# A weight group moved to ScalarE's DMA queue, and scores held until a chunk's first gate/up step

## The chip, the cores and the metric

The kernel runs on one core of one Trainium2 chip. The metric is the device time of one execution in microseconds; the median of three runs before the change is 568.12 us (567.70 to 568.79).

## The reference

The input x has 2048 tokens of width 576, in bf16. It is layer-normalised once, and two branches read the result: sliding-window attention (32 heads of 18, each token sees itself and the 255 tokens before it) and a gated feed-forward of inner width 4608.

```python
xn = _layernorm(x, axis=-1)
# attention
qkv = xn @ wqkv                       # 576 -> 3 x 576, 32 heads of 18
p = softmax(where(mask, q k^T * 18**-0.5, -1e9))
s = (p @ v) @ wo
# feed-forward
h = sigmoid(xn @ w_gate) * (xn @ w_up)   # 576 -> 4608
g = silu(h @ w_down)                     # 4608 -> 576
out = x + s * g
```

## The kernel before

**Tiling.** The tokens are done in four chunks of 512. For each chunk the kernel normalises and transposes x (`build_ln`), projects to q, k and v (`build_qkv`, matmuls on L465), and then runs the gate/up product of the feed-forward (`build_ffn`, L810), into which it weaves the attention of the same chunk: score units on L594 with their exps on ScalarE (L612), and "pv" steps, probabilities times values, on L663. Then come the attention's output product (L740) and the down product (L930). The 4608 inner columns are 36 tiles of 128, numbered from 0. One tile is 9 contraction steps, and in each step TensorE runs two matmuls side by side on its two row halves, the gate's on the lower and the up's on the upper: 18 matmuls a tile. A finished tile goes through a tanh on ScalarE (L824) into `tring`, and DVE multiplies it with the up half into `hT` (L828). Gate and up tiles use PSUM banks 4 to 7, one each, so tile n+2 needs the banks of tile n back.

**Weights.** Three gate/up tiles make a weight group. `load9` loads a group in four pieces (240, 192, 192 and 240 KB) into one of `RW` = 3 slots of `wgs`; the group after the third waits for the slot of the first, which is free when TensorE has finished tile 2. In the code `fg == RW` is this fourth group, group 3, needed from tile 9 on. At tile `XS[c]` (10 in chunk 0, 1 in the others) two of the gate's steps are done on the upper half, with their weights loaded apart into `sat` (`load_x`, "wx0"); from there on the gate of a tile ends two steps ahead of its up. A second such load, "wx1", serves the last tile.

**Queries and keys in chunk 0.** Each of the four 128-token blocks of q and of k is projected, copied to `pk` or, when that is full, to a buffer of `expr`, and then turned by a DMA transpose into `qkp` (`build_qk`, DMA line L213; plain DMAs are L214). The eight transposes go out in the order q0 q1 q2 k0 k1 q3 k2 k3, behind the third weight group (`QKT_BEHIND`). A unit of scores needs some of them; the first in TensorE's order has 16 matmuls and needs q1, q2, q3, k1 and k2.

**The order of the work.** Every DMA of the kernel before is issued from SyncE (SP). The order on each engine comes from a planner in the kernel, `schedule`. It keeps a clock for each engine and takes, on each engine, the ready operation with the least (start + 40 ns times its `prio`); a score unit has prio 1, a gate/up step 3. A DMA occupies its issuer for a fixed issue time. Its data pass through one line for all DMAs in the order of planning: it begins when the line is free, and at the earliest 1600 ns (`DMA_LAT_NS`) after its issue, and takes its (weighted) bytes at 320 a nanosecond; what needs it is ready `slack` (600 ns here) after that. `odeps` order two operations in the plan without a semaphore, `deps` with one. `emit` then writes the programs and gives every operation that somebody waits for a semaphore count; each DMA lane has a semaphore of its own. The plan's times only set the order; the chip follows the semaphores.

Due times of the plan for the kernel before, in us of the plan's clock, for following the order:

| operation | planned |
|---|---|
| third weight group, last piece landed | 26.89 |
| transposes issued, first to last | 18.84 to 27.94 |
| transpose of k2 landed, with slack | 36.10 |
| tanh of tile 2 done | 29.15 |
| gate/up tile 5 ends, tile 6 begins | 34.14 |
| first score unit starts (behind tile 6) | 36.10 |

Of the kernel before, what the change touches and what calls it, by code (L numbers as in the profile page):

```python
# [12 lines left out]
P = 128  # L13
# [21 lines left out]
RW = 3  # L35
# [10 lines left out]
RTH = 2  # L46
RREC = 2
RBN = 4
XS = (10, 1, 1, 1)
XP = (4, 0)  # L50
RUN = 3
WX_PRIO = -1
WX_FT = 7
QKV_FIRST = "q0 q1 v0 v1 q2 v2 k0 v3 k1 q3 k2 k3"
QKV_NEXT = "q0 k0 q1 v0 v1 k1 q2 k2 v2 q3 k3 v3"
QKV_GATE = 2
# [17 lines left out]
W_ISSUE_NS = 660.0  # L74
# [2 lines left out]
LATE_SLACK = 5000.0  # L77
LN_STEP = 1
XT_CUT = 4
QKT_BEHIND = {2: 0}  # L80
WARM = 10
X0_SLACK = 0.0
# [4 lines left out]
W_FACTOR = 1.42  # L87
X0_FACTOR = 1.7
XT_BYTES = 1.2
XT0_BYTES = 1.5  # L90
W0_FACTOR = 1.5
DMA_LAT_NS = 1600.0
DMA_BYTES_PER_NS = 320.0
# [6 lines left out]
def act_ns(n):  # L100
    return n / 1.2 + 80.0


def dve_ns(n, rate=1.0):
    return n / (0.96 * rate) + 75.0
# [68 lines left out]
class Builder:  # L174
# [173 lines left out]
            return r  # L348
        self.op_warm = self.pe(n * WARM_NS, f, name, deps=deps, prio=-9, psum=[ps])

    def load9(self, low, up, w_low, w_up, name, lane, deps, prio, factor):
        cols = w_low.shape[1]
        a = w_low.rearrange("(j p) c -> p j c", p=64)
        b = w_up.rearrange("(j p) c -> p j c", p=64)
        out = []
        for k, (dst, src, n) in enumerate(((low[:, 0:5, :], a[:, 0:NC:2, :], 5), (up[:, 0:4, :], b[:, 1:NC:2, :], 4),
                                           (low[:, 5:NC, :], a[:, 1:NC:2, :], 4), (up[:, 4:NC, :], b[:, 0:NC:2, :], 5))):
            out.append(self.dma(dst, src, factor * n * 64 * cols * 2, f"{name}.{k}", lane + (k,), deps=deps, prio=prio,
                                issue=W_ISSUE_NS))
        return out  # L360

    def build_weights(self):
# [399 lines left out]
    def load_x(self, c):  # L762
        self.sx, dx = self.r_s.take()
        f = XS[c] * P
        src = [(self.wg, f, 1, 64), (self.wu, (NFT - 1) * P, 0, 0)]
        self.op_wx = []
        for n, (w, f, j, r0) in enumerate(src):
            a = w[:, f:f + P].rearrange("(j p) c -> p j c", p=64)[:, j:j + 3:2, :]
            dst = self.sat[r0:r0 + 64, self.sx, 0:2 * P].rearrange("p (j c) -> p j c", j=2)
            self.op_wx.append(self.dma(dst, a, 2 * W_FACTOR * 64 * 2 * P * 2, f"wx{n}:{c}", ("wx", n), deps=dx, prio=WX_PRIO))  # L770
            self.r_s.release(self.sx, self.op_wx[-1])

    def build_ffn(self, c):
        pg = [Psum((6,), (7,), (5,), (4,)) for _ in range(NFT)]
        pu = [Psum((6,), (7,), (5,), (4,)) for _ in range(NFT)]
        slots, dmas = {}, {}
        xs, xe = XS[c], NFT - 1
        gp = [i for i in range(NC) if LO[i] not in UP[0:2]]
        up = [i for i in range(NC) if UP[i] not in LO[0:2]]
        low, high = [], []  # L780
# [3 lines left out]
        n = NC * (xs - 1) + XP[0]  # L784
        high[n:n] = [(0, xs, 0, 0), (0, xs, 1, 1)]
        n = len(low) - NC + XP[1]
# [27 lines left out]
        for n in range(len(low)):  # L814
            for half, st in enumerate((low, high)):
                gu, ft, i, x = st[n]
                count[(gu, ft)] = count.get((gu, ft), 0) + 1
                flags[(half, gu, ft, i)] = (count[(gu, ft)] == 1, count[(gu, ft)] == NC)

        def finish(ft):  # L820
            st_, dt_ = self.r_t.take()

            def f_th(e, ps=pg[ft]):
                return e.activation(self.tring[:, st_, :], self.bank(ps), ACTF.Tanh, scale=0.5)  # L824
            th = self.rd("ACT", act_ns(CH), f_th, f"th:{c}:{ft}", deps=[tile_end[(0, ft)]] + dt_, prio=1, psum=[pg[ft]])

            def f_mul(e, ps=pu[ft]):
                return e.scalar_tensor_tensor(self.hT[:, ft, :], self.tring[:, st_, :], 1.0, self.bank(ps),  # L828
                                              ALU.add, ALU.mult)
            war = [self.f2_last[ft // WDG]] if self.f2_last else []  # L830
            mul = self.rd("DVE", dve_ns(CH), f_mul, f"hm:{c}:{ft}", deps=[th, tile_end[(1, ft)]] + war, prio=1,
                          psum=[pu[ft]])
            self.r_t.release(st_, mul)
            self.op_hT[ft] = mul
# [6 lines left out]
        for n0, n1 in zip(cuts, cuts[1:]):  # L841
            deps, alloc, fence, done, ended = [prev], [], None, [], []
            for n in range(n0, n1):
                for half, st in enumerate((low, high)):
                    gu, ft, i, x = st[n]
                    fg = ft // FG
                    if x is None and fg not in slots:
                        sw, dw = self.r_w.take()
                        slots[fg] = sw
                        wp = W_PRIO[fg] if c == 0 and fg < RW else -2  # L850
                        fc = slice(fg * FG * P, (fg + 1) * FG * P)
                        ws = self.load9(self.wgs[0:64, sw, :, :], self.wgs[64:P, sw, :, :], self.wg[:, fc],
                                        self.wu[:, fc], f"w:{c}:{fg}", ("w", sw),
                                        dw + ([self.w_gate] if c > 0 and fg < RW else []), wp,
                                        W0_FACTOR if c == 0 and fg < 5 else 1.42)
                        dmas[fg] = ws
                        if c == 0 and fg == RW:
                            self.op_wx[1].add_dep(self.op_f1[(0, WX_FT)])
                        if c == 0 and fg in QKT_BEHIND:
                            for o in self.op_qkt[QKT_BEHIND[fg]:]:  # L860
                                o.behind = ws[-1:]
                    key = (gu, ft)
                    if key not in seen:
                        seen.add(key)
                        alloc.append((pg, pu)[gu][ft])
                        if self.f2_last and gu == 0:
                            deps.append(self.f2_last[ft // WDG])
                    if x is None:
                        deps += dmas[fg]
                        group_left[fg] -= 1  # L870
                        if group_left[fg] == 0:
                            ended.append(fg)
                    else:
                        deps.append(self.op_wx[gu])
                    if half != gu or key in ((0, xs), (1, xe)):
                        if tile_last.get(key, (half,))[0] != half:
                            fence = tile_last[key][1]
                    left[key] -= 1
                    if left[key] == 0:
                        done.append(key)  # L880
            if not prev:
                deps += self.all_xn

            def f(e, n0=n0, n1=n1):
                for n in range(n0, n1):
                    step(e, 0, *low[n])
                    r = step(e, 1, *high[n])
                return r
            o = self.pe((n1 - n0) * mm_ns(CH), f, f"f:{c}:{low[n0][1]}:{n0}", deps=deps, prio=3, psum=alloc, mode="r64")
            if fence:  # L890
                o.add_dep(fence)
                o.fence = fence
            for n in range(n0, n1):
                for half, st in enumerate((low, high)):
                    gu, ft = st[n][:2]
                    tile_last[(gu, ft)] = (half, o)
                    users = (pg, pu)[gu][ft].users
                    if users[-1] is not o:
                        users.append(o)
            for fg in ended:  # L900
                self.r_w.release(slots[fg], o)
            for key in done:
                tile_end[key] = o
                if key[0] == 0:
                    self.op_f1[(c, key[1])] = o
                if tile_end.get((1 - key[0], key[1])):
                    finish(key[1])
            prev = o
        for o in self.op_se:
            o.add_dep(prev)  # L910
        mms = [prev]
# [4 lines left out]
        for blocks in (((0, 1), (2,), (3,)) if c == 0 else ((0,), (1,), (2,), (3,))):  # L916
# [5 lines left out]
            for q in range(NWD):  # L922
                for i in blocks:
                    def f_f2(e, q=q, i=i, ps=banks[i]):
                        b = ps.banks[0] * 512
                        for fl in range(WDG):
                            ft = q * WDG + fl
                            lhsT = self.hT[:, ft, i * P:(i + 1) * P]
                            for n0, n1 in ((0, 512), (512, D)):
# [3 lines left out]
                    deps = [self.op_hT[ft] for ft in range(q * WDG, (q + 1) * WDG)] + [self.op_wd[q]]  # L933
                    o = self.op("PE", WDG * (mm_ns(512) + mm_ns(64)), f_f2, f"f2:{c * QPC + i}:{q}", deps, 3,
                                alloc=[banks[i]] if q == 0 else [], mode="full",
                                odeps=prev + ([self.op_wop[i - RTH]] if q == 0 and i >= RTH else []))
# [189 lines left out]
    def emit(self):  # L1126
# [8 lines left out]
        lane_cnt = [0] * len(lanes)  # L1135
        cnt = {e: 0 for e in ENGS}
        for e in ENGS:
            for o in self.prog[e]:
                if not o.needs_tok:
                    continue  # L1140
                if o.lane is not None:
                    ln = self.lane_ids[o.lane]
                    lane_cnt[ln] += 16
                    o.tok = (("L", ln), lane_cnt[ln])
                else:
                    cnt[e] += 1
                    o.tok = (("E", e), cnt[e])

        def semof(key):
            return lanes[key[1]] if key[0] == "L" else self.sem[key[1]]  # L1150
# [94 lines left out]
```

## Time and profile before

| what | value |
|---|---|
| median of three runs | 568.12 us |
| the profiled execution, its own time | 567.65 us |
| its span, first to last instruction | 565.0 us |
| granted TensorE clock | 0.999 |
| score units, L594 | 32.4 us of TensorE |
| down product, L930 | 131.0 us of TensorE |
| tanh, L824 | 144 of 600 ns on ScalarE |
| exp, L612 | 152 of 1022 ns on ScalarE |
| DMA moved over the span | 73.29 MB, mean 130 GB/s |

The profile is of one execution, and its times are us from the span's first instruction. Rows of a timeline give start, length, engine, line, operation, what is written from what, and a count; in brackets stands the idle time of that engine ahead of the row and what ended it by the profile. Engine names: PE is TensorE's matmuls, ACT ScalarE, DVE VectorE, SPq the queue of SyncE, which issues DMAs. A DMA row's length is the time of its issue, not of the transfer; "to landing" is from the issue's start to the last byte's semaphore.

### The profile page before, as it was taken

How to read it: one execution, taken by the hardware profiler on the slowest of the kernel's cores; microseconds unless marked ns; L12 is line 12 of the kernel's file. 1: busy time of each engine (PE TensorE's matmuls, PEld its weight loads, DVE VectorE, ACT ScalarE, POOL GpSimd, SP SyncE). 2: the span in 40 equal slices, each digit the busy share in tenths (PEclk: the TensorE clock that was granted, in tenths of full speed). 3: DMA queues.
4: the chain of work that ended last, by engine and by line, in shares of the span. 5: the costliest groups of instructions: out<-in, count | busy, mean ns of one | idle time of the engine just before them, and what ended most of it. 6: DMA issues, size and time to landing. Idle time of an engine off the chain costs nothing.

```text
span 565.0 us, 17870 instructions
## 1 busy us (share of the span) xinstructions
PE 555.0 (98%) x7830; PEld 283.0 (50%) x7854; DVE 307.4 (54%) x664; ACT 274.6 (49%) x372; POOL 28.2 (5%) x55
## 2 busy tenths in 40 slices
PE   8999999999999999999999999999999999999997
PEld 5634444457544444456654444445665444444544
DVE  6136987741136886772204778767121586686213
ACT  7456665514146947721407576580220855855011
POOL 3000001010000100010000011001000000000100
PEclk9999999999999999999999999999999999999999
DMA  8999999628956665324794665713559355660001
GB/s 200 219 187 249 231 224 215 136 62 114 181 105 148 151 151 135 86 52 83 106 210 109 144 153 122 161 36 71 89 124 206 87 126 129 147 131 23 20 22 43
DMA packets 126026, 73.29 MB, mean 130 GB/s; under 512 B 54782, under 2 KB 125438, under 8 KB 125950
## 3 DMA queue, kind: packets, MB, share of 16 engines
q1 hardware_dynamic: 125950, 72.16, 62.0%
q8 instruction: 62, 1.02, 0.8%
q14 instruction: 14, 0.11, 0.1%
HBM read 55.48 MB, written 2.36 MB: 102 GB/s over the span
## 4 chain that ended last, share of the span: by engine, by line
PE 94%; SPq 2%; DMA 1%; issue 1%; DVE 1%; ACT 0%
PE ps L810 50%; PE ps L930 23%; PE ps L465 8%; PE ps L594 5%; PE ps L663 4%; PE ps L740 3%; SPq L214 2%; PE ps L960 2%; DMA wqkv_sb<-in_A_wqkv_dram 1%; ACT sat L755 0%; ACT expr L612 0%; DVE tf L679 0%; DVE hT L828 0%; DVE pk L681 0%; DVE tf L684 0%
## 5 line engine op out<-in xcount | busy, mean ns | idle before, releaser
L810 PE MATMUL ps<-xn,wgs 64*128 64x512 bf16 x2576 | 296.3, 377 | 1.4 <-ACT expr L612 1.4
L810 PEld LDWEIGHTS ps<-xn,wgs 64*128 64x128 bf16 x2576 | 119.4, 94 | 143.7 <-issue 8.9
L612 ACT ACTIVATE expr<-ps 128x1024 bf16<-128x1024 f32 x152 | 147.2, 1022 | 26.3 <-PE ps L594 26.1
L930 PE MATMUL ps<-wd_sb,hT 128*128 128x64 bf16 (+1 forms) x1056 | 131.0, 284 | 2.2 <-issue 1.0
L824 ACT ACTIVATE tring<-ps 128x512 bf16<-128x512 f32 x144 | 86.3, 600 | 82.8 <-PE ps L810 80.6
L828 DVE SCALAR_TENSOR_TENSOR hT<-tring,ps 128x512 bf16<-128x512 bf16 x144 | 97.9, 680 | 30.6 <-ACT tring L824 14.2
L930 PEld LDWEIGHTS ps<-wd_sb,hT 128*128 128x128 bf16 x1080 | 68.1, 98 | 65.0 <-issue 1.4
L630 DVE TENSOR_TENSOR expr<-expr,m 128x512 bf16<-128x512 bf16 (+2 forms) x152 | 58.5, 412 | 55.5 <-ACT expr L612 54.5
L991 ACT ACTIVATE thf<-ps 128x576 bf16<-128x576 f32 (+2 forms) x17 | 10.6, 622 | 135.5 <-PE ps L930 128.3
L993 DVE SCALAR_TENSOR_TENSOR thf<-thf,ps 128x576 bf16<-128x576 bf16 (+2 forms) x17 | 12.2, 719 | 106.5 <-ACT thf L991 106.5
L465 PE MATMUL ps<-wqkv_sb,xn 64*128 64x288 bf16 x864 | 54.7, 283 | 0.5 <-ACT xn L454 0.2
L465 PEld LDWEIGHTS ps<-wqkv_sb,xn 64*128 64x128 bf16 x864 | 42.9, 94 | 11.2 <-issue 1.8
L594 PEld LDWEIGHTS ps<-qkp 18*64 18x64 bf16 x1472 | 16.2, 103 | 32.6 <-ACT expr L612 14.0
L594 PE MATMUL ps<-qkp 18*64 18x320 bf16 (+4 forms) x1472 | 32.4, 259 | 0.1
L641 POOL COPY qkp<-qkp 128x256 bf16<-128x256 bf16 x24 | 9.8, 410 | 288.1 <-PE ps L594 288.1
L513 DVE CAST pk<-ps 128x576 bf16<-128x576 f32 x15 | 11.3, 755 | 23.1 <-PE ps L465 22.9
L703 DVE STREAM_TRANSPOSE op__63<-pk 128x512 bf16<-128x512 bf16 x32 | 22.3, 698 | 0.2
L663 PEld LDWEIGHTS ps<-expr,vau 64*32 64x32 bf16 x1440 | 18.0, 92 | 7.6 <-issue 4.9
L681 DVE STREAM_TRANSPOSE pk<-ps 128x512 f32<-128x512 f32 x32 | 21.5, 673 | 0.0
L663 PE MATMUL ps<-expr,vau 64*32 64x320 bf16 (+5 forms) x1440 | 20.9, 253 | 0.3
L740 PE MATMUL ps<-wo_sb,oT 64*128 64x512 bf16 (+1 forms) x288 | 18.7, 283 | 0.1
L679 DVE STREAM_TRANSPOSE tf<-ps 128x512 f32<-128x512 f32 x16 | 11.5, 716 | 11.8 <-PE ps L663 11.8
(54 smaller groups left out, 197.1 us busy)
## 6 DMA issues: line engine op xcount, KB each, us to landing
wgs<-in_B_w_gate_dram SPq DMA_DIRECT2D x48, 240.0 KB, 3.9
wgs<-in_B_w_up_dram SPq DMA_DIRECT2D x48, 240.0 KB, 4.9
wgs<-in_B_w_up_dram SPq DMA_DIRECT2D x48, 192.0 KB, 4.0
wgs<-in_B_w_gate_dram SPq DMA_DIRECT2D x48, 192.0 KB, 4.8
wd_sb<-in_B_w_down_dram SPq DMA_DIRECT2D x9, 576.0 KB, 8.2
xf<-in_A_x_dram SPq DMA_DIRECT2D x18, 144.0 KB, 2.2
out_dram<-xf SPq DMA_DIRECT2D x15, 144.0 KB, 2.0
xr<-in_A_x_dram SPq DMA_DIRECT2D x14, 144.0 KB, 4.7
```

What stands on the lines that cost most here:

```text
L465: r = e.matmul(self.bank(ps, HV, hf), self.xn[r0:r0 + 64, k, i * P:(i + 1) * P], self.wqkv_sb[r0:r0 + 64, j, k, :], start=(k == 0), stop=( ...
L594: r = e.matmul(self.ps[64 * half:64 * half + 64, b:b + n * 64], self.qkp[r0:r0 + DH, hg, k0:k0 + 64], self.qkp[r0:r0 + DH, hg, q0 * 64:(q0 ...
L612: return e.activation(self.expr[:, es, 2 * pr:2 * pr + 2, :], src, ACTF.Exp, scale=SM_SCALE)
L630: return e.tensor_tensor(ap, ap, m, ALU.mult)
L663: r = e.matmul(self.ps[32 * j:32 * j + 32, b + q0 * 64:b + (q0 + n) * 64], vf[:, v0:v0 + 32], self.expr[p0:p0 + 64, es, j, pos * 64:(pos + ...
L681: t3 = self.rd("DVE", dve_ns(CH), lambda e, tg=tg, hg=hg: e.transpose(tg, self.bank(ps2[hg][1])), f"t3:{c}:{hg}", deps=[o, self.last_mul] ...
L703: t2 = self.op("DVE", dve_ns(CH), lambda e, on=on: e.transpose(self.op_[:, hg % NOT, :], on.rearrange("p g d -> p (g d)")), f"t2:{c}:{hg}" ...
L740: r = e.matmul(self.bank(ps2[w], n1 - n0, n), self.oT[r0:r0 + 64, kt, qi * P:(qi + 1) * P], self.wo_sb[r0:r0 + 64, kt, n0:n1], start=(swap ...
L810: return e.matmul(self.bank((pg, pu)[gu][ft]), w, self.xn[r0:r0 + 64, i, :], start=first, stop=last, tile_position=(r0, 0))
L824: return e.activation(self.tring[:, st_, :], self.bank(ps), ACTF.Tanh, scale=0.5)
L828: return e.scalar_tensor_tensor(self.hT[:, ft, :], self.tring[:, st_, :], 1.0, self.bank(ps), ALU.add, ALU.mult)
L930: r = e.matmul(self.ps[:, b + n0:b + n1], lhsT, self.wd_sb[:, q, fl, n0:n1], start=(ft == 0), stop=(ft == NFT - 1))
```

## The change

Group 3 of chunk 0 is issued from ScalarE: the first two pieces are ordered after the tanh of tile 2, the other two after that of tile 3. `XS[0]` goes from 10 to 13, and wx0 now waits for the end of gate tile 5 (wx1 for that of tile 7, as before). The planner's byte factor for the transposes of chunk 0, `XT0_BYTES`, goes from 1.5 to 1.2. In chunks 1 to 3 every score unit is ordered after the chunk's first gate/up step (`SC_GATE`). Semaphore counts of DMA lanes are given in the order of the plan over all engines, since a lane may now be used from two engines.

```diff
-XS = (10, 1, 1, 1)
+XS = (13, 1, 1, 1)
-WX_FT = 7
+SC_GATE = 0
-XT0_BYTES = 1.5
+XT0_BYTES = 1.2
@@ load9
-    def load9(self, low, up, w_low, w_up, name, lane, deps, prio, factor):
+    def load9(self, low, up, w_low, w_up, name, lane, deps, prio, factor, eng="SP"):
...
-                                issue=W_ISSUE_NS))
+                                issue=W_ISSUE_NS, eng=eng))
@@ build_ffn
+        ths = {}
...
+            ths[ft] = th
...
-                                        W0_FACTOR if c == 0 and fg < 5 else 1.42)
+                                        W0_FACTOR if c == 0 and fg < 5 else 1.42, "ACT" if c == 0 and fg == RW else "SP")
                         dmas[fg] = ws
                         if c == 0 and fg == RW:
-                            self.op_wx[1].add_dep(self.op_f1[(0, WX_FT)])
+                            self.op_wx[0].add_dep(self.op_f1[(0, 5)])
+                            self.op_wx[1].add_dep(self.op_f1[(0, 7)])
+                            for k, o in enumerate(ws):
+                                o.odeps.append(ths[2 + k // 2])
...
             prev = o
+            if n0 == SC_GATE and c > 0:
+                for l in self.op_sc[c]:
+                    for u in l:
+                        u.odeps.append(o)
@@ emit
-                if o.lane is not None:
-                    ln = self.lane_ids[o.lane]
-                    lane_cnt[ln] += 16
-                    o.tok = (("L", ln), lane_cnt[ln])
-                else:
+                if o.lane is None:
                     cnt[e] += 1
                     o.tok = (("E", e), cnt[e])
+        for o in sorted((o for o in self.ops if o.lane is not None), key=lambda o: o.idx):
+            ln = self.lane_ids[o.lane]
+            lane_cnt[ln] += 16
+            o.tok = (("L", ln), lane_cnt[ln])
```

More of the change, by code (lines that the diff above doesn't have):

```diff
@@ L769, in load_x @@
             dst = self.sat[r0:r0 + 64, self.sx, 0:2 * P].rearrange("p (j c) -> p j c", j=2)
-            self.op_wx.append(self.dma(dst, a, 2 * W_FACTOR * 64 * 2 * P * 2, f"wx{n}:{c}", ("wx", n), deps=dx, prio=WX_PRIO))
+            self.op_wx.append(self.dma(dst, a, 2 * W_FACTOR * 64 * 2 * P * 2, f"wx{n}:{c}", ("wx", n), deps=dx, prio=WX_PRIO,
+                                       eng="SP"))
             self.r_s.release(self.sx, self.op_wx[-1])
```

## The prediction

> **What bounds the kernel now.** I read the page first: engine shares, then the groups with the idle time before each.
>
> ```profile
> span 565.0 us, 17870 instructions
> ...
> PE 555.0 (98%) x7830; PEld 283.0 (50%) x7854; DVE 307.4 (54%) x664; ACT 274.6 (49%) x372; POOL 28.2 (5%) x55
> ...
> L810 PE MATMUL ps<-xn,wgs 64*128 64x512 bf16 x2576 | 296.3, 377 | 1.4 <-ACT expr L612 1.4
> ```
>
> TensorE is the bound; the matmuls themselves are not changed, so the change can only take away or add TensorE idle time. The gate/up line L810 has 1.4 us of it, the only wait over 0.3 us after the start-up. Next I read TensorE's timeline at that place.
>
> ```profile
> 33.70 2.75 PE L810 MATMUL ps<-xn,wgs 64*128 64x512 bf16 x24
> 36.55 0.42 PE L594 MATMUL ps<-qkp 18*64 18x320 bf16 x16
> 36.90 3.19 PE L810 MATMUL ps<-xn,wgs 64*128 64x512 bf16 x28
> 40.03 0.43 PE L594 MATMUL ps<-qkp 18*64 18x64 bf16 x24
> 40.39 1.04 PE L810 MATMUL ps<-xn,wgs 64*128 64x512 bf16 x8
> 42.79 1.04 PE L810 MATMUL ps<-xn,wgs 64*128 64x512 bf16 x8 [1.37 <-ACT expr L612]
> ```
>
> Count the gate/up matmuls, 18 to a tile: 10 before 19.3, 116 up to 36.55, then 28 and 8 make 162, nine tiles. So the 1.37 us stand ahead of tile 9, the first of the fourth weight group. ACT is named as releaser, but its exp had long been issued; SyncE's queue shows the real one.
>
> ```profile
> 14.38 0.62 SPq L214 DMA_DIRECT2D sat<-in_B_w_gate_dram  x1
> ...
> 20.33 7.47 SPq L213 DMA_TRANSPOSE qkp<-pk  x3
> 27.85 7.86 SPq L213 DMA_TRANSPOSE qkp<-expr  x5
> 35.76 0.60 SPq L214 DMA_DIRECT2D wgs<-in_B_w_gate_dram  x1
> ...
> 37.73 0.62 SPq L214 DMA_DIRECT2D wgs<-in_B_w_up_dram  x1
> ```
>
> The fourth group's slot is free once tile 2 is done (its tanh starts at 28.73), yet its four pieces stand behind eight transposes and are issued from 35.76 on. The last, issued at 37.73, takes 4.7 to land (the tile's own view): 42.4, and tile 9 starts at 42.79. The last view is the landing of the seventh transpose (key block 2), alone in its window, with the DMA rate in 40 slices of 0.45 us from 28 to 46.
>
> ```profile
> L213 SPq DMA_TRANSPOSE qkp<-expr x1: 1393/1393/1393, 32.0 to 32.0; - x1
> ...
> DMA to landing us min/median/max: 4.4/4.4/4.4
> ```
>
> ```profile
> GB/s 225 199 178 212 202 150 213 204 154 214 207 142 240 38 3 9 162 274 233 191 58 147 362 236 224 188 232 234 230 203 218 217 205 230 210 236 201 240 211 217
> ```
>
> It lands at 36.4, and the first score unit (16 matmuls, needing query blocks 1 to 3 and key blocks 1 and 2) starts at 36.55: no slack at all. From 33.85 to 35.2 (38, 3, 9) the DMA hardly moves, while two transposes are on the way; I call this the lull.
>
> **The change, part by part.**
>
> *Group 3 from ScalarE.* The stall ahead of tile 9 goes: issued after tanh 2 and 3 (28.73 and 30.67, 0.60 each), the four pieces go out at about 29.4 to 32.6. With the 6.1 us that the slowest of the pieces issued from 37.7 to 40.4 takes to land, they are in by 38.7, before 41.43. Gain 1.37. They wait only for the end of tile 2, as tanh 2 ahead of them does. ScalarE pays four issues; SyncE's rows give 0.62 each. Two fit in the 1.34 it sits idle between tanhs. Queued behind them are tanh 3 and 4, for which DVE waits and then the PSUM banks of tiles 5 and 6. Tile 3's product would be done at 32.0 and tile 5 starts at about 32.65, so some 0.6 of delay is covered. No row shows an issue on ScalarE: between 0 and twice SyncE's price costs TensorE 0 to 0.6. I take 0.
>
> *The planner's byte factor of chunk 0's transposes, 1.5 to 1.2.* No instruction changes, but the order does. By the planner's formula a transpose takes 8x128x128x2x1.5/320 = 1229 ns of its DMA line, after it 983. On the plan's clock (the due times of the section on the kernel; they set the order and are no forecast) the weights ahead end at 26.89; without the 0.29 of the side load below, at 26.60. Seven transposes later key block 2 lands at 33.48, with the 600 ns slack at 34.08; before it was 36.10. Group 3 is issued from 29.17 on that clock, when all eight transposes are already placed (the last at 27.50), so it is queued behind them and doesn't push them back. Tile 5 ends at 34.14 there, and a ready score unit goes ahead of a gate/up step. So the unit moves **one tile earlier**, from behind tile 6 to behind tile 5. On the chip a tile is 1.95 (tanhs are 1.94 apart), so TensorE stands before it at 36.55 - 1.95 = 34.60.
>
> *What it then waits for.* This is the new wait, and gate/up tile 6 and all that follows is queued behind it. Its price is when key block 2 lands. (a) At best: the issue moves with the drain of the weights, 0.26 earlier (the side load landed at 14.38 + 5.0 = 19.4, the piece ahead at 19.1), so 31.73; an unhindered transpose lands 3.3 after its issue (the third, at 26.49); 0.15 from landing to start as now: 31.73 + 3.3 + 0.15 - 34.60 = **0.6**. (b) With the lull as now: 36.4 - 0.26 + 0.15 - 34.60 = **1.7**. (c) Group 3 is now on the way beside the transposes. It is 864 KB, and at the 220 GB/s of the weight stretches that is 4.0 us of all DMA engines. All of it ahead of key block 2 gives 5.7, the upper end. I take three quarters (the first two pieces whole, half of the other two), 3.0, less 1.35 that run in the lull and 0.45 that fit beside issue-bound transposes (about 200 of 280 GB/s over 1.5 us): 1.7 + 1.2 = **2.9**, near (b), the nearest row.
>
> The row for this sharing: in the stretches from 28 to 32 the DMA share of the profile is already 1.08 and 0.97. The Trainium skill, page "DMA: Bandwidth & Descriptors", section "Issuing engines are not separate DMA queues", says that DMAs from scalar and sync run on the same 16 engines and interleave, so that a second issuer saves only issue time; it speaks against a free ride. By it alone the sum would use (c)'s upper end and come to +4.3; by the lull's row alone it would use (b) and come to +0.3. No row of this case has two issuers.
>
> *The side load for tile 10, now 13, and held until tile 5.* Its 0.62 on SyncE at 14.38 goes; that is the 0.26 above. At its new place SyncE has only loads that are due much later: 0. Until tile 12 gate and up tiles now end together. Tile 8 (end 41.43, tanh 42.42, product to 43.92) would hold back a tile 10 due at 43.74 by 0.2; at most four tiles, so 0 to 0.8. I take 0.1.
>
> *Scores held until the chunk's first gate/up step.* In chunks 1 to 3 the first score unit already stands behind a full tile (162.26, after 18 gate/up matmuls from 160.21): 0.
>
> *Semaphore counts by planned order.* No instruction: 0.
>
> Sum: -1.37 - 0.09 (today's gap ahead of the first unit) + 2.9 + 0.1 = **+1.5**. The profiled execution took 567.65 (span 565.0, 2.65 around it), so 569.2; it lies 0.47 under the median 568.12, to which I add the same: **569.6**.
>
> **The rivals.** *The transposes are hardly disturbed*: (a) to 1.0, because the lull doesn't recur or group 3 fills only it. Then -0.8 to -0.4 after the 0.1 for banks, 567.3 to 567.7. For it: 4.0 us of load against a 1.35 lull and spare DMA; against it: share near 1. Chance 0.12.
> *The unit doesn't wait*: one place, the first score unit. If it keeps its place behind tile 6, or key block 2 lands by 34.45, only the gain is left: -1.46, **566.7**, faster. It decides at plan time 34.22: were key block 2 due later than that, the unit would stay. My margin there is 0.14; and with a landing of 36.1 the unit at 36.55 waits for nothing. Against it: (a). Chance 0.18.
> *ScalarE's issues stand behind the transposes' own* (1.31 to 1.39 each on SyncE): then tanh 3 and 4 come up to 2 us late, and banks and transposes with them: +2.2 to +4, 570.3 to 572. Chance 0.10.
> The forecast has the rest, 0.60, from (b) to 4.0 of wait: +0.3 to +2.6.
>
> **How the numbers follow.** About 0.2%, 1.14 us, is what a measurement here can tell from no change. Faster: the second rival, 0.18. Within: the first, 0.12, and of the forecast the waits under 2.5, 0.18: 0.30. Slower: the rest of the forecast, 0.42, and the last rival: 0.52. The range, 566.8 to 571.0, leaves out the lower half of the second rival and the top of the last; the forecast's own is 568.4 to 570.7.
>
> **What would show it.** Four weight issues on ScalarE at 29.4 to 32.6; the first score unit after 108 gate/up matmuls, with a TensorE gap of about 2.9 from 34.6; key block 2 landing near 37.3; no gap ahead of tile 9; chunks 1 to 3 unchanged, only shifted. I am wrong if the unit stands behind 126 matmuls, if its gap is under 1.4, or if tanh 3 is late by over 0.6.

## The result, and the profile after

The changed kernel takes 573.52 us (median of 6 runs, 572.37 to 574.35), the kernel before 567.91 on the same chip (6 runs, 566.59 to 568.79): a ratio of 1.0098, 95% interval 1.0079 to 1.0117. It is slower by 5.6 us, where 1.5 were forecast, and the time lies above the range, which ended at 571.0. The profiled execution took 572.41 (span 570.2, 2.2 around it); its span is 5.2 longer than before's.

The page of the changed kernel, in which the gate/up line has become L811:

```profile
span 570.2 us, 17898 instructions
...
PE 558.9 (98%) x7854; PEld 283.6 (50%) x7854; DVE 308.1 (54%) x664; ACT 274.6 (48%) x372; POOL 28.6 (5%) x55
...
L811 PE MATMUL ps<-xn,wgs 64*128 64x512 bf16 x2576 | 297.5, 378 | 0.3 <-DVE hT L831 0.3
...
L594 PE MATMUL ps<-qkp 18*64 18x320 bf16 (+4 forms) x1472 | 32.6, 261 | 5.6 <-DMA qkp<-expr 5.6
```

Read the last columns against those of before: the gate/up line had 1.4 us of idle time ahead of it and has 0.3; the score line L594 now has 5.6, released by a transpose into `qkp`. TensorE's busy time is up by 3.9 us, but 2.9 of that are a hole in the record: the trace of before has 7854 weight loads and only 7830 matmuls, and the 24 that it lacks are of the down product (L930 x1056, 131.0 us; here L941 x1080, 133.9). The gate/up line is complete in both, 2576 matmuls, and is up from 296.3 to 297.5: some of them ran longer. TensorE's timeline shows where:

```profile
23.29 10.81 PE L811 MATMUL ps<-xn,wgs 64*128 64x512 bf16 x98
39.66 0.65 PE L594 MATMUL ps<-qkp 18*64 18x320 bf16 x16 [5.56 <-DMA qkp<-expr]
40.25 4.46 PE L811 MATMUL ps<-xn,wgs 64*128 64x512 bf16 x28
44.64 0.43 PE L594 MATMUL ps<-qkp 18*64 18x64 bf16 x24
45.00 2.98 PE L811 MATMUL ps<-xn,wgs 64*128 64x512 bf16 x26
47.91 0.43 PE L594 MATMUL ps<-qkp 18*64 18x64 bf16 x24
48.69 2.12 PE L811 MATMUL ps<-xn,wgs 64*128 64x512 bf16 x18 [0.34 <-DVE hT L831]
```

With the 10 gate/up matmuls ahead of these rows, the first score unit stands behind 108, six tiles. TensorE idles for 5.56 us ahead of it, from 34.10. Then 28 gate/up matmuls take 4.46 (3.19 before) and the 16 of the unit 0.65 (0.42). Tile 9 (the last row) no longer waits for weights; 0.34 of waiting for a PSUM bank stands there.

Three stretches of the windows view after the gap, and two of before at the same place (columns: window, its length, busy time of PE, PEld, DVE, ACT and POOL, then the granted clock, DMA share and GB/s):

```profile
39.60:41.00 1.40, 1.34 (x20) 0.52 (x22) 0.00 (x0) 0.62 (x1) 0.00 (x0) 0.50 0.93 236
41.00:43.00 2.00, 2.00 (x12) 0.76 (x10) 0.62 (x2) 1.32 (x2) 0.00 (x0) 0.54 1.07 224
43.00:45.00 2.00, 2.00 (x40) 0.90 (x37) 0.79 (x2) 0.60 (x1) 0.00 (x0) 1.00 0.67 133
```

```profile
36.00:38.00 2.00, 1.91 (x34) 0.69 (x30) 0.69 (x1) 1.50 (x3) 0.00 (x0) 1.00 0.88 174
38.00:40.00 2.00, 2.00 (x20) 0.77 (x16) 0.93 (x3) 1.57 (x3) 0.00 (x0) 1.00 1.07 242
```

The granted clock is half from 39.4 to 42.8, 3.4 us, then full again. In before it stays at 1.00 here. The profiled execution has one such stretch, and a granted clock of 0.997 over all; four of the six had 0.993 to 0.994 (573.28 to 574.35 us). Half clock for 3.4 of 570 us is 0.003 of the clock, so by this estimate those four had two such stretches, which can explain why the median lies 1.1 us above the profiled execution.

The seventh transpose (key block 2), alone in its window, and the DMA rate in 40 slices of 0.45 us from 28 to 46, as shown of before:

```profile
L213 SPq DMA_TRANSPOSE qkp<-expr x1: 1617/1617/1617, 32.0 to 32.0; - x1
...
  PE ps L594: 5.6, 1
...
DMA to landing us min/median/max: 7.5/7.5/7.5
```

```profile
GB/s 181 197 208 176 42 97 339 246 129 185 356 259 205 196 253 206 267 280 204 172 20 5 10 184 283 290 170 222 316 253 201 186 234 265 201 83 23 161 161 0
```

Issued at 32.01, it lands at 39.53; before it took 4.4 us. The DMA engines are busy nearly all the time from 30.5 to 37. Group 3's pieces land at 32.44, 34.27, 35.68 and 38.66, all four ahead of key block 2; of the transposes only that of key block 1 lands between 30.3 and 38.8 (34.62). The lull (20, 5, 10) is still there, from 37.0 to 38.4. The two queues share the engines. From 31 to 35.5 the DMA view has as many bytes for SyncE's queue (q1), which carries the transposes, as for ScalarE's (q10):

```profile
q1 hardware_dynamic: 2080, 0.52, 78.2%
q10 hardware_dynamic: 707, 0.51, 45.2%
```

The columns are packets, MB and the share of 16 engines' time.

Chunk 1's projections start at 129.71 (before 124.59): +5.12. Those of chunks 2 and 3 are shifted by 5.11 and 5.14. So all of it arises in chunk 0:

| term | us |
|---|---|
| first score unit at 39.66, against 34.60, its place before moved up by one tile | +5.06 |
| half clock: first to second score unit 4.98, against 3.48 | +1.50 |
| bank wait ahead of tile 9 | +0.34 |
| stall ahead of tile 9 | -1.37 |
| sum | +5.53 |

The 0.4 over +5.12 lies in one pv step: that of before at 73.63 takes 1.52, where the others of 72 matmuls in chunk 0 take 1.11 or 1.12, in both executions.

### The profile page after: what moved, and what is told of

Its sections match the earlier page's. It is cut to its first block, busy times and chain, and to the rows that moved or that the text cites. A ratio compares the mean times of both kernels' runs of the same rounds, so it can differ in the third digit from the quotient of the medians.

```text
span 570.2 us, 17898 instructions
## 1 busy us (share of the span) xinstructions
PE 558.9 (98%) x7854; PEld 283.6 (50%) x7854; DVE 308.1 (54%) x664; ACT 274.6 (48%) x372; POOL 28.6 (5%) x55
## 4 chain that ended last, share of the span: by engine, by line
PE 96%; DMA 2%; DVE 1%; issue 0%; ACT 0%; SPq 0%; ACTq 0%
PE ps L811 50%; PE ps L941 23%; PE ps L465 9%; PE ps L594 5%; PE ps L663 3%; PE ps L740 3%; PE ps L971 2%; DMA qkp<-expr 1%; DMA xr<-in_A_x_dram 0%; PE ps L444 0%; ACT expr L612 0%; DVE bnst L408 0%; DVE bnst L410 0%; DVE hT L831 0%; DVE expr L630 0%
## 5 line engine op out<-in xcount | busy, mean ns | idle before, releaser
L811 PE MATMUL ps<-xn,wgs 64*128 64x512 bf16 x2576 | 297.5, 378 | 0.3 <-DVE hT L831 0.3
L811 PEld LDWEIGHTS ps<-xn,wgs 64*128 64x128 bf16 x2576 | 120.3, 94 | 143.3 <-issue 9.1
L941 PE MATMUL ps<-wd_sb,hT 128*128 128x512 bf16 (+1 forms) x1080 | 133.9, 286 | 0.0
L941 PEld LDWEIGHTS ps<-wd_sb,hT 128*128 128x128 bf16 x1080 | 68.1, 98 | 65.0 <-issue 1.4
L465 PEld LDWEIGHTS ps<-wqkv_sb,xn 64*128 64x128 bf16 x864 | 42.5, 94 | 11.1 <-issue 1.1
L594 PE MATMUL ps<-qkp 18*64 18x320 bf16 (+4 forms) x1472 | 32.6, 261 | 5.6 <-DMA qkp<-expr 5.6
L594 PEld LDWEIGHTS ps<-qkp 18*64 18x64 bf16 x1472 | 16.2, 103 | 38.1 <-issue 18.3
```

What stands on the lines that cost most here:

```text
L465: r = e.matmul(self.bank(ps, HV, hf), self.xn[r0:r0 + 64, k, i * P:(i + 1) * P], self.wqkv_sb[r0:r0 + 64, j, k, :], start=(k == 0), stop=( ...
L594: r = e.matmul(self.ps[64 * half:64 * half + 64, b:b + n * 64], self.qkp[r0:r0 + DH, hg, k0:k0 + 64], self.qkp[r0:r0 + DH, hg, q0 * 64:(q0 ...
L811: return e.matmul(self.bank((pg, pu)[gu][ft]), w, self.xn[r0:r0 + 64, i, :], start=first, stop=last, tile_position=(r0, 0))
L941: r = e.matmul(self.ps[:, b + n0:b + n1], lhsT, self.wd_sb[:, q, fl, n0:n1], start=(ft == 0), stop=(ft == NFT - 1))
```

## The experiments

The theory: the data of group 3, now on a second queue beside the transposes, no longer wait for them; key block 2 is late by their whole time, and the gap that follows is long enough to bring the clock down. The rivals: the unit's earlier place makes the wait by itself (first); a second issuing engine disturbs the transposes, whatever it moves (second); the half clock is no consequence of the gap (third). All kernels are edits of the changed kernel. The kernel before was run beside them on the same chip: its median was 568.4 us beside the runs with group 3 back on SyncE, with few bytes, with the unit behind tile 6 and with the gap filled, 568.1 beside the last two, and 568.3 beside the others. The ratios are to these.

**Group 3 back on SyncE.** All else stays: unit one tile earlier, side load 13, wx0 held.

```
-  ..., "ACT" if c == 0 and fg == RW else "SP")
+  ..., "SP")
-                            for k, o in enumerate(ws):
-                                o.odeps.append(ths[2 + k // 2])
```

> Group 3 back on SyncE's queue behind the transposes, all else as after the change (first score unit still behind tile 5). Theory: the 5.56 us wait is mostly group 3's data beside the transposes, so key block 2 lands near 36.0 again, the gap ahead of the unit is 1.7 to 2.0, the clock stays full, and tile 9 (due at about 42.8) hardly waits for its weights: 568.2 us (567.6 to 569.0). Rival 1, the earlier place alone makes the wait: gap near 5.5 and about 573.5 us.

Measured: 567.25 (7 runs), ratio 0.9986, 0.9960 to 1.0012; span 564.4. Its timeline:

```profile
35.18 0.42 PE L594 MATMUL ps<-qkp 18*64 18x320 bf16 x16 [0.43 <-DMA qkp<-expr]
35.73 3.20 PE L811 MATMUL ps<-xn,wgs 64*128 64x512 bf16 x28
...
42.90 2.12 PE L811 MATMUL ps<-xn,wgs 64*128 64x512 bf16 x18 [0.34 <-ACT tring L827]
```

```profile
L213 SPq DMA_TRANSPOSE qkp<-expr x1: 1323/1323/1323, 31.7 to 31.7; - x1
...
DMA to landing us min/median/max: 3.3/3.3/3.3
```

Key block 2 lands at 35.04 and the unit waits 0.43; the clock stays at 1.00. The expectation had the landing near 36.0 and 567.6 at the least: the lull that it counted on did not come among these transposes. The first rival falls: the earlier place costs some 0.4. The second queue, with the lull that the changed kernel has and this execution hasn't, costs some 5. Tile 9 waits for no weights either, though SyncE still issues group 3 behind the eight transposes (its last piece lands at 42.25): the transposes are through earlier, and one score unit more stands ahead of tile 9.

**Group 3 from ScalarE with few bytes.** The four issues stay where the change put them, but each moves 16 of its 384 columns.

```
+            if eng == "ACT":
+                dst, src = dst[:, :, 0:16], src[:, :, 0:16]
```

> Group 3 is issued from ScalarE as after the change, four DMAs with the same rows, but only 16 of 384 columns each (1/24 of the bytes); tiles 9 to 11 so compute mostly with the first group's weights. Theory (bytes): key block 2 lands near 36, gap 1.7 to 2.5, 568.2 us (567.5 to 569.2). Rival 2 (a second issuer by itself holds up the transposes, whatever it moves): gap 4 or more, 571.5 us or more.

Measured: 567.51 (8 runs), ratio 0.9981, 0.9967 to 0.9995.

```profile
36.19 0.42 PE L596 MATMUL ps<-qkp 18*64 18x320 bf16 x16 [1.48 <-DMA qkp<-expr]
```

Key block 2 lands at 36.05, the unit waits 1.48, and the clock stays up. The second rival falls: with four issues from a second engine, but next to none of their bytes, the kernel isn't slower than before. Of the 5.1 by which the unit's wait grew, the second issuer by itself can explain 1.0 at most (1.48 against 0.43); the rest goes with the bytes and the lull. (Group 3's smaller load also takes some 4 us of DMA time off the loads behind it, so the 0.9 us under before isn't to be had.)

**Group 3 from ScalarE with half the bytes.** The same, with 192 columns.

> As the run with few bytes, but 192 of the 384 columns, half the bytes of group 3 in the same rows, from ScalarE after tanh 2 and 3 (tiles 9 to 11 compute partly with the first group's weights). Theory (the transposes wait for the bytes): key block 2 lands between the 36.05 of few bytes and the 39.53 of all, near 37.8, up to 1.5 later if a lull falls in; gap ahead of the unit 3 to 4.5; 570.0 us (568.7 to 571.5). Rival (it is a threshold or the lull alone): as few bytes, 567.5, or as all, 573.5.

Measured: 571.31 (8 runs), ratio 1.0053, 1.0034 to 1.0072.

```profile
39.12 0.65 PE L596 MATMUL ps<-qkp 18*64 18x320 bf16 x16 [4.80 <-DMA qkp<-expr]
```

Key block 2 lands at 38.99, the gap is 4.80, the half clock lasts from 37.0 to 43.8. The order of the times is few, half, all, as the theory has it, but a lull of 1.5 us (36.5 to 38) fell into this execution's transposes, so its gap can't be read as bytes alone.

**The first score unit one tile later again**, behind tile 6, with group 3 on ScalarE.

```
-            if n0 == SC_GATE and c > 0:
+            if n0 == 59 and c == 0:
+                self.op_sc[0][0][0].odeps.append(self.op_sc[0][0][1])
+            if n0 == (59 if c == 0 else SC_GATE):
```

> As after the change, but the first score unit is held until tile 6 is done (its old place); group 3 still on ScalarE. Theory: key block 2 lands at 39.5 as after the change, TensorE arrives 1.95 later, gap 3.6; the clock falls again if 3.6 idle is enough: 571.5 us, or 570.0 if the clock stays full. Rival (the unit waits for something that moves with it): gap stays 5.5, 573.5 us.

Measured: 572.44 (4 runs), ratio 1.0063, 1.0040 to 1.0087.

```profile
40.61 0.65 PE L594 MATMUL ps<-qkp 18*64 18x320 bf16 x16 [4.14 <-DMA qkp<-expr]
```

The gap was 4.14, not 3.6, since key block 2 landed at 40.48 in this execution, 1 us later than in the changed kernel; the clock fell for 3.4 us again. By the ratios (1.0063 against 1.0098) the old place takes back some 2 us, the tile that now runs ahead of the wait, though the two intervals touch. The transposes come too late for either place.

**The gap filled.** 24 matmuls of 128x128x512, which are not part of the computation, run ahead of the first score unit.

```
...
+                for k in range(24):
+                    r = e.matmul(self.bank(ps), self.hT[:, 0, 0:P], self.hT[:, 0, :], start=True, stop=True)
...
```

> As after the change, with 24 extra matmuls (128x128x512, result overwritten) between tile 5 and the first score unit, which keep TensorE busy for about 5.2 of the 5.56 us. Theory: the unit starts at the same 39.7 but the clock stays at 1.0, so the 28 matmuls behind it take 3.1 instead of 4.46: 1.5 to 2.3 us less, 571.5 us. Rival 3 (those matmuls are slow for another reason, such as DMA traffic): no gain, 573.5 us.

Measured: 572.96 (4 runs), ratio 1.0072, 1.0051 to 1.0094. The timeline, in which L608 is the filling (23 of its 24 matmuls are in the trace) and L821 the gate/up line:

```profile
34.83 5.13 PE L608 MATMUL ps<-hT 128*128 128x512 bf16 x23 [0.16 <-issue]
41.47 0.42 PE L594 MATMUL ps<-qkp 18*64 18x320 bf16 x16 [1.51 <-DMA qkp<-expr]
41.95 3.20 PE L821 MATMUL ps<-xn,wgs 64*128 64x512 bf16 x28
```

The clock stays at 1.00, the 28 matmuls take 3.20 instead of 4.46, and the unit its 0.42: the third rival falls, the half clock comes from the idle time. All four executions had a clock of 0.999 or 1.000, the changed kernel's six 0.993 to 0.997. From the first unit to the second it is 3.61 instead of 4.98, a gain of 1.37. The ratio fell from 1.0098 to 1.0072, about as much, but the two intervals overlap, and key block 2 landed at 41.33 in this execution, 1.8 later. Of that, 1.1 stood before the filling began, at the landing of the fourth transpose (31.40 against 30.30); the other 0.7 is not explained.

**Group 3 from ScalarE, two tiles later**: pieces 0 and 1 ordered after the tanh of tile 4, the others after that of tile 5. Their planned bytes are set to 1, so that the plan doesn't move the transposes for them.

```
-                                o.odeps.append(ths[2 + k // 2])
+                                o.odeps.append(ths[4 + k // 2])
+                                o.nbytes = 1.0
```

> Group 3 still on ScalarE's queue with all its bytes, but after tanh 4 and 5 instead of 2 and 3 (the planner is told that it has no bytes, so that the first unit keeps its place behind tile 5). Its data then start near 34.2, when key block 2 is almost in. Theory: gap ahead of the unit 0.4 to 1.5 (key block 2 at 35.0 to 36.0), weights of tile 9 in by 40.5, no gap there; 567.5 us (566.8 to 568.5). Rival 2 (a second issuer harms whenever it runs): 571 us or more.

Measured: 570.52 (5 runs), ratio 1.0051, 1.0032 to 1.0070: a miss of 3 us. The profiled execution was the longest of the five, 572.66. ScalarE's and TensorE's timelines, key block 2's transpose, and what the two queues moved from 35.5 to 37.5:

```profile
32.55 0.72 ACTq L214 DMA_DIRECT2D wgs<-in_B_w_gate_dram  x1
33.31 0.66 ACTq L214 DMA_DIRECT2D wgs<-in_B_w_up_dram  x1
```

```profile
38.06 0.42 PE L594 MATMUL ps<-qkp 18*64 18x320 bf16 x16 [3.61 <-DMA qkp<-expr]
38.61 5.75 PE L811 MATMUL ps<-xn,wgs 64*128 64x512 bf16 x36
```

```profile
L213 SPq DMA_TRANSPOSE qkp<-expr x1: 1316/1316/1316, 32.3 to 32.3; - x1
...
DMA to landing us min/median/max: 5.6/5.6/5.6
```

```profile
q10 hardware_dynamic: 546, 0.40, 109.2%
q1 hardware_dynamic: 56, 0.01, 3.2%
```

This miss tells most. Only two pieces, 432 KB, are issued while key block 2 is on the way, and after the issue of its transpose, the seventh of the eight, had begun (32.28). The other two stand on ScalarE behind the first unit's exp and go out at 38.55 and 39.19. At 220 GB/s the two pieces are 2.0 us of all DMA engines. Key block 2 would have landed at 35.6 by the pace of the three ahead of it (3.3 us from issue to landing each); it lands at 37.92, after the first piece (37.58) and ahead of the second (38.55). The delay is 2.3 us, with no lull in this execution. So these data cost a transpose whose issue had begun before theirs their whole time; no part of it fits beside. The gap of 3.61 brought the clock to half from 39.1 to 42.5, too.

One measure sets the runs side by side. The fourth transpose lands before any piece of group 3 does, at 30.2 to 31.6, so the time from its landing to that of key block 2 leaves out how late an execution got there:

| group 3 beside the transposes | fourth transpose to key block 2, us | lull, us |
|---|---|---|
| none: SyncE, three executions (two of them below) | 4.08, 4.15, 4.18 | none |
| none: the kernel before | 5.26 | 1.4 |
| ScalarE, 36 KB | 4.44 | none |
| ScalarE, 432 KB: two pieces, later | 6.45 | none |
| ScalarE, 432 KB: half of each piece | 7.99 | 1.5 |
| ScalarE, 864 KB: the changed kernel | 9.22 | 1.4 |
| ScalarE, 864 KB: unit behind tile 6 | 9.23 | 1.3 |
| ScalarE, 864 KB: gap filled | 9.93 | 0.5 |

Without a lull, 432 KB cost 2.3. With a lull of 1.4, 864 KB cost 3.96 (9.22 against 5.26), and at 220 GB/s they are 4.0. So bytes and lull add up, and the lull comes without a second queue, too. The 1.0 by which the run with the unit behind tile 6 was later than the changed kernel had all arisen before the fourth transpose landed.

**Key blocks 1 and 2 earlier**, group 3 on SyncE: the transposes of query block 0 and key blocks 0 and 3 get a later priority in the plan.

```
-                      ..., deps=[ev] + old, prio=0,
+                      ..., deps=[ev] + old, prio=2 if c == 0 and (i, j) in ((0, 0), (0, 1), (3, 1)) else 0,
```

> As group 3 on SyncE with the early unit, but the transposes of q0, k0 and k3 go last, so the five that the first unit needs go first; the planner then puts the unit behind tile 4. Theory: key block 2 lands at about 32.3 to 32.8, TensorE is there at 32.6, gap under 0.4, the second unit waits little; 567.0 us, 0.1 to 0.3 percent under the kernel before. Rival (something else of 0.4 or more takes its place): 567.5 to 568.5.

Measured: 574.17 (6 runs), ratio 1.0101, 1.0078 to 1.0124. The first unit indeed waits for nothing, but the second waits 1.64 for key block 3, and the shifted plan put loads of the down projection ahead of a weight group:

```profile
103.04 0.61 PE L811 MATMUL ps<-xn,wgs 64*128 64x512 bf16 x4 [3.82 <-DMA wgs<-in_B_w_up_dram]
```

That gap of 3.82 again halves the clock (104.6 to 108.0). The transposes did as expected, the time did not: the planner answered with another order of DMAs far behind the place that was edited.

**The side load back at 10**, group 3 on SyncE.

```
-XS = (13, 1, 1, 1)
+XS = (10, 1, 1, 1)
```

> Group 3 on SyncE with the early unit, and the side load back at tile 10 (loaded after tile 5, as after the change). Theory: the 0.34 gap ahead of tile 9 comes from tanh and banks and is not changed by the side load's tile, so this is within 0.5 us of the run with tile 13, 567.2 to 567.8 us. Rival: with tile 10 the gate ends two steps ahead sooner, and the gaps behind tile 9 go, up to 0.5 us faster.

Measured: 570.79 (4 runs), ratio 1.0048, 1.0029 to 1.0067. The theory and the rival both missed. The side load, held until tile 5 as in the change, lands at 46.23, and its first matmuls now stand in the tenth tile (number 9):

```profile
46.28 0.60 PE L811 MATMUL ps<-xn,wgs 64*128 64x512 bf16 x1 [1.90 <-DMA sat<-in_B_w_gate_dram]
```

With two further gaps of 0.43 and 0.69, 3.0 us of idle time within 4.5, the clock went to half here as well (45.6 to 49.1). So with the hold, 10 is too early a place; 10 without the hold was not run on top of this change.

**Group 3 on SyncE once more, with more runs, alone and with key block 0's transpose last.** The first is the kernel of the first experiment once more; the second has this besides:

```
+                      ..., prio=2 if c == 0 and (i, j) == (0, 1) else 0,
```

> The same kernel as group 3 on SyncE with the early unit, once more with more rounds, to see whether it beats the kernel before. Its TensorE gaps were 0.43 ahead of the first unit and 0.34 ahead of tile 9, against 1.37 and 0.09 before: 0.7 to 1.2 us under the kernel before, 567.2 us; a lull of up to 1.5 us in the transposes would eat it in some executions. Rival: no difference, 568.0.

> The same with the transpose of k0 last, so key block 2 is the sixth: the planner puts the unit into the middle of tile 5. Theory: no gap ahead of the unit (key block 2 at 33.7), but TensorE then reaches tile 9 about 0.5 sooner, while its weights land at 42.2 as before, so up to 0.5 of wait comes there: within 0.4 us of the run above, 567.0 to 567.5. Rival: the 0.43 are won outright, 566.7 or less.

Measured: 567.55 (12 runs), ratio 0.9995, 0.9981 to 1.0008; and 567.33 (12 runs), ratio 0.9997, 0.9983 to 1.0012. Neither can be told from the kernel before. Their profiles say why the 1.37 us aren't won: in the first the unit waits 0.98 (key block 2 lands at 35.38) and tile 9 still waits 0.68 for its weights (the last piece lands at 43.23 and the tile starts at 43.58, 0.35 later, as in before: 42.44 and 42.79); in the second the first unit waits 0.61 and the second 1.07, for key block 0, which lands last (38.69). Half of the stall ahead of tile 9 stayed in the first, and the rest became waits elsewhere.

Holding the scores of chunks 1 to 3 wasn't run alone: without it the kernel gives the same program, instruction for instruction.

## Why the prediction was right and wrong

- **The stall ahead of tile 9 goes** (-1.37): right; no row of the changed kernel has it. The prediction's reason for setting the exp aside was loose, since that exp ran until 42.55, but its reading holds: the last piece landed at 42.44 and tile 9 started 0.35 later, and the same 0.35 stands in the second run with group 3 on SyncE.
- **ScalarE's issues cost nothing**: right. They were forecast at 29.4 to 32.6, and stand at 28.32 to 31.7:

```profile
28.31 0.60 ACT L827 ACTIVATE tring<-ps 128x512 bf16<-128x512 f32 x1 [1.34 <-PE ps L811]
28.32 0.71 ACTq L214 DMA_DIRECT2D wgs<-in_B_w_gate_dram  x1
29.06 0.64 ACTq L214 DMA_DIRECT2D wgs<-in_B_w_up_dram  x1
30.25 0.60 ACT L827 ACTIVATE tring<-ps 128x512 bf16<-128x512 f32 x1 [1.35 <-PE ps L811]
```

  The issue starts with the tanh, not at its end, and takes 0.61 to 0.78; the tanhs stay 1.94 to 1.95 apart. The rival in which the issues hold up the tanhs is out.
- **The unit moves one tile earlier**: right, 108 matmuls, so the second rival is out. The unhindered landing of (a), 31.73 + 3.3 = 35.0, is that of the run with group 3 on SyncE: 35.04.
- **What it then waits for: here the forecast failed**, at the words "three quarters (the first two pieces whole, half of the other two), 3.0, less 1.35 that run in the lull and 0.45 that fit beside issue-bound transposes". That priced group 3 beside the transposes at 1.2 and put the landing at 37.3. All four pieces landed ahead of key block 2, and it came at 39.53. Counted from the fourth transpose they cost it 3.96, the whole 4.0 of their time, and neither deduction held. The lull wasn't filled: it came after most of the data, at 37.0, on top of them. And little fitted beside the transposes: from 30 to 37 the engines moved 219 GB/s in all, while the transposes by themselves ran at 191 (group 3 on SyncE, 28.5 to 35) and the weights at the prediction's 220. In the prediction's count, from 34.60, the wait is 5.06. Its (c) had 5.7; the 0.6 between them is that the transposes ran earlier than it had them, the fourth landing 0.85 ahead of before's (30.30 against 31.15) where it counted 0.26. So the upper end stood in the prediction, but the forecast's waits went to 4.0 only, and the range ended below it.
- **The order of the data.** In the plan group 3 stands behind all eight transposes, because the planner's line takes the DMAs one by one in planned order. On the chip the two queues ran side by side, 0.52 and 0.51 MB from 31 to 35.5. The Trainium skill, "DMA: Bandwidth & Descriptors", section "Issuing engines are not separate DMA queues", which the prediction weighed, says that DMAs from different issuers interleave on the same 16 engines and that a second issuer saves issue time alone. The trace agrees: with two queues at work the engines moved 219 GB/s in all from 30 to 37, no more than the weights alone.
- **A term that was missing: the clock.** The sum priced a gap at its length. The gaps of 5.56, 4.80, 4.14, 3.82 and 3.61 were each followed by a half clock, for 3.4 us or more; those of 1.37 (before), 1.48, 1.51 and 1.64 weren't. Worth 1.50 here, 1.37 by the run with the filling. The Trainium skill, "TensorE: Matmul & The Clock Gate", Part 1, says that the clock falls after an idle window of about 3.4 us. The traces agree only roughly: with half the bytes it fell 2.7 us after TensorE had gone idle (34.3 to 37.0), and 3.0 us of idle time in three pieces did it, too. No gap between 1.9 and 3.6 was run by itself, so the runs don't give the point.
- **Banks** (0.1, bounds 0 to 0.8): 0.34, in the bounds, though ahead of tile 9, which waits for the banks of tile 7 (product done at 48.54, tile at 48.69), and not of tile 10.
- **Chunks 1 to 3 only shifted**: right, to 0.03.

Of the error of 3.6 us (+5.12 against +1.5), 2.25 are the wait (5.06 against the 2.81 that the sum had after its 0.09), 1.50 the clock and 0.24 the banks; the 0.4 of the pv step goes off. The rival with an undisturbed transpose is refuted by the size of the gap.

## What to carry to other kernels

Ahead of moving a load to an idle engine's queue, ask which small, urgent DMA is on the way at that time: the move takes nothing off the DMA engines, and here 864 KB that used to stand behind eight transposes landed ahead of the last three of them, and the wait that this made, with the lull in it, is four times the stall that it removed. A planner that treats all DMAs as one line in order doesn't see this. Where the engine that sets the end would idle for several microseconds, add the time at the lower clock that follows. And a stall that is removed is only worth what the next wait leaves: the version without the second queue takes away half of the same stall or all of it, and can't be told from the kernel before.

## What the runs showed of the hardware

- DMA transposes and loads of another queue share the engines, in stretches very unevenly: in the changed kernel each queue moved 0.5 MB from 31 to 35.5, but in the run with two pieces later the transposes moved 0.01 MB from 35.5 to 37.5 and the loads 0.40. With two pieces of 240 and 192 KB issued behind it, a transpose landed 5.6 us after its issue instead of 3.3; in the changed kernel one took 8.8 (query block 3, 30.07 to 38.88).
- The lull has a companion. In each profile with a lull of the kind shown, 0.5 to 1.5 us long and begun after the fifth transpose has landed (before, the changed kernel, and the runs with the unit behind tile 6, with the filling, with half the bytes and with key blocks 1 and 2 earlier), a 16 KB packet of the instruction queue, 0.9 to 1.6 us long, starts 0.3 to 1.5 us ahead of it: in before at 33.56 and the lull from 33.85, in the changed kernel at 36.27 and 37.0. In the two runs with group 3 on SyncE it came at 37.01 and 37.92, after the last transpose had landed, and no lull followed. In the run with key block 0 last it came at 36.48, with only that transpose on the way, which landed 5.1 after its issue instead of 3.3. Every profile has such a packet at 21.8 to 24.9, too, and a stretch under 50 GB/s 0.7 to 3 us behind its start, among the first transposes (before: 23.03, and 26.0 to 26.5). Not every dip has one: in the changed kernel the DMA moved 27 GB/s from 29.9 to 30.5, as group 3's first piece set in, with no packet ahead. That the packet causes the delay was not tried, and what sets its time is open.
- ScalarE's queue issues a DMA while its own ACTIVATE is running: 28.32 beside a tanh from 28.31 to 28.91.
- Every stretch of full or half clock that lies wholly inside a trace is a whole multiple of 3.41 us long, one or two at half, so the change comes at points of its own: at half clock from 37.0, 2.7 us into the gap, with half the bytes, and from 104.6, 1.6 us after the gap's end, with key blocks 1 and 2 earlier. In 8 of the 53 executions of the kernel before that were run beside the experiments the granted clock was 0.996 or 0.997 as well; no trace of these eight is kept, and what they waited for is not known.
